# Unread matmuls in TensorE's waits through the whole head, held weight stores, GpSimd casts and a last store on ScalarE's queue

## The chip, the cores and the metric

The kernel runs on one core of a Trainium2 chip. The metric is device time in microseconds of one execution. The time before is the median of three runs, 546.33 us (545.79 to 549.88).

## What is computed

Three blocks follow each other on a tensor of 2 batches, 768 positions and 512 channels (8 heads of 64):

```python
# windowed attention with a linear distance bias
keep = (pos_k < n_global) | ((rel >= 0) & (rel < n_local))     # n_global 8, n_local 96
a = softmax(where(keep, q @ k.T / 8 - slope[h] * dist, -1e9))
x = (a @ v) in the layout batch, position, channel
# layer norm and a channel MLP of 2048
x = x + relu(norm(x) * g_ln @ w_ch1) @ w_ch2
# token MLP of 256, then a channel MLP of 1536
u = x + (relu(x.T @ w_tok1) @ w_tok2).T
out = u + relu(u @ w_ch1) @ w_ch2
```

## The kernel before, in words

The 12 tiles of 128 positions (x0 to x11, `NTT` = 12) stay in SBUF as f32. `window_tile` (line 400) makes one attention tile: scores of two heads at a time (line 452, f32 matmuls), a biased minimum on VectorE (line 467), the exponential on ScalarE (line 472), a transposition on TensorE (line 477), a copy of the transposed probabilities out of PSUM (line 525, on ScalarE or VectorE as `EVX` says) and the product with V (line 482, f32, for tiles below `SPLIT` = 6; later tiles split the operands into f16 pairs). `norm_ops` does the layer norm and `turn_ops` turns a normed tile by a transposing DMA (line 591). `mlp_ops` is the channel MLP: every product is three f16 matmuls (`mm3`, lines 372 to 374: high by high, high by low, low by high). Groups are of three tiles; the first product with weights (buffers `L` from `xa`, `wa`) needs all three turned tiles of group 0.

The weights arrive as 64-bit words. `Weights.split` loads them (line 166, staging `stg`), casts the top half on ScalarE (line 755, into `fw`), joins it with the shifted lower words on VectorE (line 761, into `wf`), and makes a high half (line 777, ScalarE) and a low half (line 780 on GpSimd or line 783 on VectorE). `Weights.get` stores each finished pair of the channel MLPs to a scratch in DRAM (line 736, 256 KB) and reads it back for later passes (line 726). Nearly all DMAs are issued in order by SyncE (SP), so one whose semaphore hasn't come holds all those behind it.

The order of the instructions is not written by hand. `Plan` simulates the engines with a cost for every operation, a priority, and a latency per engine (`LAT`), and emits the operations in that order. The priorities come from constants (`AHEAD`, `SLOT`, `HEAD`, `DUE`, `EARLY`, `LEAD`, `STORE`, `RELOAD`), and strings such as `LOA1`, `EVX` and `MK1` say which engine takes which operation. In the simulation TensorE runs at half rate when too little was done in the window before, apart from the windows in `WARM`, which are taken as done. In `emit`, until the end of the `WARM` windows, unread matmuls of a zero tile (`keep_busy`, line 106, 256 columns, 0.11 us each in the plan) fill a gap that the simulation shows ahead of a TensorE operation. `WARM` is (1, 8), which ends 22.4 us after the plan's zero; the last such matmuls stand at 26.0 us of the trace. An operation of no cost in `rest` ends the filling; it waits for the second turned tile of group 0. The setup ahead of the plan issues 10 and 3 of them (`BUSY`).

In tiles below `SPLIT`, the first 32 rows of the V and K slots are refilled with the global positions after a tile's last product (lines 546 and 548), since the next tile reads that slot again: from that product to the data's arrival the plan takes 1.2 us (`ISSUE`), 0.3 us for the DMA and 1.8 us (`LAT["S"]`).

`distances` (line 110) and `masks` build the bias tables at the start. `Guard.__init__` writes limits and ones by small GpSimd memsets. At the end the addition of the last tile (a "tail" operation) and the stores of tiles 10 and 11 (`BEHIND`) are issued in a last block on SP, ahead of a branch that repeats all in another precision if the guard's sums say so.

Of the kernel before, what the change touches and what calls it, by code (L numbers as in the profile page):

```python
# [182 lines left out]
class Plan:  # L183
# [3 lines left out]
    LAT = {"T": 0.2, "V": 0.13, "A": 0.15, "G": 0.1, "S": 1.8, "N": 0.0}  # L187
# [212 lines left out]
def window_tile(o, plan, prio, T, slot):  # L400
# [40 lines left out]
    for p in range(4):  # L441
# [88 lines left out]
        if T < SPLIT:  # L530
            op("T", 2 * PVC * n, prio(k + slot["PV"]), pv, r=[(pt, 0), *vkeys], w=[(bvs[p // 2], p % 2)], get=bvs if p == 0 else [])
# [20 lines left out]

    if T >= SPLIT:
# [90 lines left out]
class Guard:  # L644
# [7 lines left out]
    def __init__(self, o, plan):  # L652
        self.o, self.plan = o, plan
        self.n = {k: v[0] for k, v in self.AT.items()}
        nc = o.nc
        c = o.check = o.gp.tile([P, 3, self.N], F32, name="check")
        o.ones = o.gp.tile([P, 2], F32, name="ones2")
        o.half1 = o.gp.tile([P, 3], F16, name="half1")
        o.cnt = o.gp.tile([P, 6], F32, name="cnt")
        o.junk = o.gp.tile([P, 512], BF16, name="junk")  # L660
        for k, (a, b, lo, hi) in self.AT.items():
            for i, y in ((1, lo), (2, hi)):
                plan.op("G", 0.2, GUARD0, lambda i=i, a=a, b=b, y=y: nc.gpsimd.memset(c[:, i, a:b], y), w=[("lim", k, i)])
        for i, y in enumerate((1.0, TINY)):
            plan.op("G", 0.2, GUARD0, lambda i=i, y=y: nc.gpsimd.memset(o.ones[:, i:i + 1], y), w=[("one", i)])
        plan.op("A", 0.3, GUARD0, lambda: nc.scalar.activation(out=o.half1[:, 0:2], in_=o.ones[:], func=AF.Copy), r=[("one", 0), ("one", 1)], w=[("half", 0)])
        plan.op("V", 0.1, GUARD0, lambda: nc.vector.tensor_copy(o.half1[:, 2:3], o.ones[:, 1:2]), r=[("one", 1)], w=[("half", 1)])
# [46 lines left out]
class Weights:  # L714


    def __init__(self, o, plan, keep):
        self.o, self.plan, self.kept, self.keep, self.seen = o, plan, set(), keep, set()

    def get(self, src, prio):  # L720
# [12 lines left out]
        if src[0] in self.keep:  # L733
# [3 lines left out]
            op("S", 1.46, prio + STORE, store, r=[(b, "h"), (b, "l")], w=[("kept", src)])  # L737
# [3 lines left out]
    def split(self, src, prio, dst, key, get=(), r=(), after=()):  # L741
# [342 lines left out]
LOA1 = 'VGGGGGVVVVVVGGGV'
LOB1 = 'GVGVVVVGVGVVVVGV'
LOA2 = 'GGVGGGVVGVGV'
LOB2 = 'VGGGVGGGGVGV'
LOT = 'VVG'
NLO, ULO = 'GGGVVVGGVVVV', 'GGVVVVGVVVGG'
# [53 lines left out]
def rest(o, ctx, attn, fast):  # L1143
# [36 lines left out]
    if fast:  # L1180
        plan.WARM = (1, 8)
# [98 lines left out]
LEADS, FLEAD = -94.61, 405.4  # L1280
F2LEAD = [-24.45, -24.48]
FE, SE = 'VGGVVGVVGGVG', 'GVGVGVVG'
HEAD = 72.86
DUE = [38.89, 17.63, 79.14, 46.98]
EARLY = [-33.75, -24.73, -1.92, 0.28]
LEAD = -148.51
EVAC = 19.77
TOK1 = 19.62
TOKW, TOK0 = 157.31, 177.61
# [5 lines left out]
class WindowAttention:  # L1295
# [8 lines left out]
    def ops(self, o, plan, prio):  # L1304
# [16 lines left out]
        for T in range(1, NTT):  # L1321
            window_tile(o, plan, lambda k, T=T: prio(T, k), T, SLOT)
# [5 lines left out]
class GeneralAttention:  # L1328

# [81 lines left out]
def mixer_kernel(ctx, tc, q, k, v, n_global, n_local, g_ln, w1, w2, wt1, wt2, w3, w4, out):  # L1411
# [20 lines left out]
    near = nc.values_load(flag[0:1, 0:1], min_val=0, max_val=1)  # L1432
# [5 lines left out]
    again = nc.values_load(o.again[0:1, 0:1], min_val=0, max_val=1)  # L1438
# [50 lines left out]
```

## Time and profile before

| what | us |
| --- | --- |
| median of three runs | 546.33 |
| lowest and highest run | 545.79, 549.88 |
| the profiled execution's own time | 550.31 |
| its span in the trace | 548.5 |
| TensorE busy in the span | 536.9 |

The profile names engines PE (TensorE matmuls), PEld (its weight loads), DVE (VectorE), ACT (ScalarE), POOL (GpSimd) and SP (SyncE). PEclk is the clock that TensorE was granted as a share of 2.4 GHz: 0.50 is 1.2 GHz. Matmuls are pipelined, so the durations of several in a row overlap. The stretches of time named below are from the start of the span.

### The profile page before, as it was taken

What the parts mean: (1) busy time and instruction counts of PE and PEld (TensorE: products, weight loads), DVE (VectorE), ACT (ScalarE), POOL (GpSimd) and SP (SyncE); (2) the same over time, 40 slices, a digit from 0 to 9 for tenths busy, and PEclk for the clock granted to TensorE, in tenths of its full rate; (3) what the DMA queues carried; (4) which work ended last, traced back from release to release, by engine and by line L of the source; (5) the groups of instructions that cost most, each with busy time, mean ns of one, the idle gap of its engine ahead of it and who ended that gap; (6) DMA issues with size and microseconds to landing.
All of it is one profiled execution on the core that took longest, in us unless ns stands there. A gap on an engine that the chain in (4) does not pass through costs nothing.

```text
span 548.5 us, 9023 instructions
## 1 busy us (share of the span) xinstructions
PE 536.9 (98%) x3117; PEld 303.2 (55%) x3117; DVE 399.9 (73%) x856; ACT 343.1 (63%) x765; POOL 189.1 (34%) x203
## 2 busy tenths in 40 slices
PE   8989999999999999999999999999999999999995
PEld 6877755656565555554555454454555545554542
DVE  6875895588599875787878877888797786654431
ACT  6987976678776744659875736566855554624210
POOL 2232320134022212456344348534544763231000
PEclk9986999999999999999999999999999999999999
DMA  8895996688968777943775610134893332202012
GB/s 260 246 241 161 258 258 173 200 260 247 291 148 218 163 211 203 334 156 95 201 234 173 214 61 3 56 134 136 212 257 124 125 129 98 75 0 78 2 39 81
DMA packets 99786, 89.94 MB, mean 164 GB/s; under 512 B 59028, under 2 KB 73364, under 8 KB 99732
## 3 DMA queue, kind: packets, MB, share of 16 engines
q1 hardware_dynamic: 99730, 89.29, 56.4%
q8 instruction: 26, 0.43, 0.3%
q14 instruction: 28, 0.23, 0.1%
q10 hardware_dynamic: 2, 0.00, 0.0%
HBM read 61.87 MB, written 17.83 MB: 145 GB/s over the span
## 4 chain that ended last, share of the span: by engine, by line
PE 91%; ACT 3%; DVE 2%; DMA 2%; issue 0%; POOL 0%; ACTq 0%; POOLq 0%
PE L L372 12%; PE L L374 12%; PE L L373 12%; PE L2S L374 9%; PE L2S L373 9%; PE L2S L372 8%; PE S L452 4%; PE k L372 4%; PE k L374 4%; PE k L373 4%; PE k L482 4%; PE T L477 3%; PE tok L373 2%; PE tok L374 2%; PE tok L372 2%; DMA stg<-in_moe_w_ch_dram 1%
## 5 line engine op out<-in xcount | busy, mean ns | idle before, releaser
L372 PE MATMUL L2S<-wb,h 128*128 128x512 f16 x228 | 86.4, 379 | 0.0
L373 PE MATMUL L2S<-wb,h 128*128 128x512 f16 x228 | 86.4, 379 | 0.0
L374 PE MATMUL L2S<-wb,h 128*128 128x512 f16 x228 | 86.4, 379 | 0.0
L900 DVE SCALAR_TENSOR_TENSOR x<-L2S,x 128x512 f32<-128x512 f32 x57 | 39.2, 688 | 45.0 <-PE L2S L374 44.8
L374 PEld LDWEIGHTS <-h 128*128 128x128 f16 x336 | 32.9, 98 | 39.6
L372 PEld LDWEIGHTS <-h 128*128 128x128 f16 x336 | 32.9, 98 | 36.5 <-issue 1.0
L373 PEld LDWEIGHTS <-h 128*128 128x128 f16 x336 | 32.9, 98 | 35.5
L755 ACT ACTIVATE fw<-stg 128x512 f16<-128x512 bf16 x62 | 47.1, 776 | 8.6 <-DMA stg<-in_moe_w_ch_dram 6.1
L834 POOL TENSOR_TENSOR Q<-Q 128x256 f32<-128x256 f32 x36 | 31.9, 885 | 47.1 <-DVE Q L834 47.1
L761 DVE SCALAR_TENSOR_TENSOR wf<-stg,fw 128x512 uint32<-128x512 uint32 x62 | 45.7, 750 | 2.5 <-ACT fw L755 2.4
L472 ACT ACTIVATE ex<-ex,mn 128x256 f32<-128x256 f32 (+1 forms) x96 | 41.8, 482 | 8.0 <-DVE mn L467 7.9
L467 DVE CUSTOM_DVE_ANT_0 ex<-bmh,S 128x256 f32<-128x256 bf16 x80 | 30.4, 415 | 15.1 <-PE S L452 11.3
L372 PE MATMUL L<-wb,h 128*128 128x512 f16 x108 | 41.0, 379 | 0.0
L373 PE MATMUL L<-wb,h 128*128 128x512 f16 x108 | 40.9, 379 | 0.0
L374 PE MATMUL L<-wb,h 128*128 128x512 f16 x108 | 40.9, 379 | 0.0
L834 POOL TENSOR_TENSOR sz<-Q,sz 128x512 f16<-128x512 f32 x18 | 23.7, 1318 | 44.7 <-ACT sz L926 40.6
L372 PEld LDWEIGHTS <-wa 128*128 128x128 f16 x268 | 26.4, 98 | 19.0 <-issue 1.3
L374 PEld LDWEIGHTS <-wa 128*128 128x128 f16 x268 | 26.2, 98 | 17.5 <-DVE wa L783 0.3
L373 PEld LDWEIGHTS <-wa 128*128 128x128 f16 x268 | 26.2, 98 | 17.2
L372 PE MATMUL L<-xa,wa 128*128 128x384 f16 x104 | 34.0, 327 | 0.0
L374 PE MATMUL L<-xa,wa 128*128 128x384 f16 x104 | 33.9, 326 | 0.0
L373 PE MATMUL L<-xa,wa 128*128 128x384 f16 x104 | 33.9, 326 | 0.0
(237 smaller groups left out, 1359.7 us busy)
## 6 DMA issues: line engine op xcount, KB each, us to landing
stg<-in_moe_w_ch_dram SPq DMA_DIRECT2D x56, 512.0 KB, 5.1
wa<-scr_1a SPq DMA_DIRECT2D x24, 256.0 KB, 4.4
wb<-scr_1b SPq DMA_DIRECT2D x24, 256.0 KB, 4.1
scr_1a<-wa SPq DMA_DIRECT2D x16, 256.0 KB, 4.6
scr_1b<-wb SPq DMA_DIRECT2D x16, 256.0 KB, 5.0
K<-in_k_dram SPq DMA_DIRECT2D x12, 256.0 KB, 3.7
Q<-in_q_dram SPq DMA_DIRECT2D x12, 256.0 KB, 4.0
V<-in_v_dram SPq DMA_DIRECT2D x12, 256.0 KB, 5.2
```

The source lines that it names most:

```text
L372: nc.tensor.matmul(ps, ah, bh, start=first, stop=False, **k)
L373: nc.tensor.matmul(ps, ah, bl, start=False, stop=False, **k)
L374: nc.tensor.matmul(ps, al, bh, start=False, stop=last, **k)
L452: nc.tensor.matmul(bs[j].t[:, i, :w], o.Q[r, qs, p + i, :], o.K[r, slots, p + i, :], start=True, stop=True)
L467: nc.vector.tensor_tensor_reduce(out=ex.t[:, j, :w], in0=o.bm0[:, h] if n == 1 else o.bmh[:, h, ms, :], in1=bs[j].t[:, p % 2, :w], scale=- ...
L472: nc.scalar.activation(out=ex.t[:, j, :w], in_=ex.t[:, j, :w], func=AF.Exp, bias=mn.t[:, h:h + 1], scale=-1.0)
L477: nc.tensor.transpose(bt.t[:, j, i, :], ex.t[:, j, i * P:(i + 1) * P], o.ident[:])
L482: nc.tensor.matmul(bv.t[:, 2 * (p % 2) + j], pt.t[:, j, i, :], o.V[:, z, 2 * p + j], start=(i == 0), stop=(i == n - 1))
L755: op("A", 0.66, prio - 2, lambda: nc.scalar.activation(out=fw.t[:, :, 1], in_=stg.t[:, 4:2049:4].bitcast(BF16), func=AF.Copy, scale=2.0 if ...
L761: op("V", 0.6, prio - 1, lambda: nc.vector.scalar_tensor_tensor(out=raw().bitcast(U32), in0=stg.t.bitcast(U32)[:, 1:1024:2], scalar=13, in ...
L834: op(eng, {"G": 0.1 + n * 0.00227, "V": 0.07 + n * 0.00104}[eng], prio, lambda: e.tensor_tensor(out=out(), in0=a(), in1=b(), op=alu), lock ...
L900: n = op("V", 0.6, prio, lambda: nc.vector.scalar_tensor_tensor(out=x[:], in0=b.t[:], scalar=BACK if o.half else 1.0, in1=x[:], op0=ALU.mu ...
```

## The change

- `WARM` goes from (1, 8) to (1, 16), so that the fillers may stand until 49.7 us after the plan's zero, and the operation that ends them waits for the third turned tile of group 0. `BUSY` goes from 10 and 3 to 8 and 4.
- `LAT["S"]` goes from 1.8 to 2.4 us.
- Stores of weights to the scratch wait for the last product of tile 4 (`W.hold`, `LATE` = 3).
- Eight of the 32 casts of line 755 for the first channel MLP go to GpSimd (`FA1`, `FB1`), three of them among the first 16.
- `distances` clips only the last 128 columns before the branch; the other 384 are clipped later in `distant`. The guard's memsets and those of `vb` come after tile 0's last minimum.
- The store of tile 10 is issued ahead of the last addition, that of tile 11 on ScalarE's queue.
- Two loads of a register from a tile come without a check of their range at run time.
- All constants of the plan are new, so the order of the whole program is another one. `EVX` gives the copies of tile 3 to VectorE.

```diff
-    t = tp.tile([P, 4 * P], F32, name="mt")
+    t = o.x[NTT - 4]
...
-    nc.vector.tensor_tensor(out=rel[:], in0=rel[:], in1=t[:], op=ALU.max)
+    nc.vector.tensor_tensor(out=rel[:, 3 * P:], in0=rel[:, 3 * P:], in1=t[:, 3 * P:], op=ALU.max)
...
-    LAT = {"T": 0.2, "V": 0.13, "A": 0.15, "G": 0.1, "S": 1.8, "N": 0.0}
+    LAT = {"T": 0.2, "V": 0.13, "A": 0.15, "G": 0.1, "S": 2.4, "N": 0.0}
...
-                plan.op("G", 0.2, GUARD0, lambda i=i, a=a, b=b, y=y: nc.gpsimd.memset(c[:, i, a:b], y), w=[("lim", k, i)])
+                plan.op("G", 0.05, GUARD0, lambda i=i, a=a, b=b, y=y: nc.gpsimd.memset(c[:, i, a:b], y), r=[("first", 3, 1)], w=[("lim", k, i)])
...
-            op("S", 1.46, prio + STORE, store, r=[(b, "h"), (b, "l")], w=[("kept", src)])
+            op("S", 1.46, prio + STORE, store, r=[(b, "h"), (b, "l")], w=[("kept", src)], after=self.hold)
...
+            top = lambda: stg.t[:, 4:2049:4].bitcast(BF16)
+            if o.half and src[0] == 1 and (FA1 if src[1] == "a" else FB1)[src[2]] == "G":
+                op("G", 1.65, prio - 2, lambda: nc.gpsimd.tensor_scalar(
+                    out=fw.t[:, :, 1], in0=top(), scalar1=2.0 if wide else 1.0, scalar2=None, op0=ALU.mult),
+                   r=[(stg, 0), ("zeros",)], w=[(fw, 0)], get=[fw])
...
-STORE, RELOAD = 44.56, -3.32
+STORE, RELOAD = 41.58, 14.54
...
+FA1 = 'AGGAAAAGAAGAAAGA'
+FB1 = 'AAAAAAAAGGAAAAGA'
...
-BUSY = 10, 3
+BUSY = 8, 4
...
-EVX = 'AAAAAAAAAAAV'
+EVX = 'AAAVAAAAAVAA'
...
-        plan.WARM = (1, 8)
+        plan.WARM = (1, 16)
...
     attn.ops(o, plan, prio)
+    W.hold = attn.done[LATE:LATE + 1]
...
-        plan.op("T", 0.0, 0.0, lambda: setattr(plan, "busy", lambda n: None), r=[(g[0], 1, "h")], w=[(idle, 0)])
+        plan.op("T", 0.0, 0.0, lambda: setattr(plan, "busy", lambda n: None), r=[(g[0], 2, "h")], w=[(idle, 0)])
...
+        store(o, BEHIND[0])
         for x in rest:
             x.fn()
-        for T in BEHIND:
-            store(o, T)
+        store(o, BEHIND[1], "scalar")
...
+        def distant():
+            sl = slice(0, 3 * P)
+            nc.vector.tensor_tensor(out=o.bmt[:, sl], in0=o.bmt[:, sl], in1=o.x[NTT - 4][:, sl], op=ALU.max)
+            may(o, o.bmt, o.col, o.x[NTT - 1][:, sl], 0, 3, False)
+        plan.op("V", 1.7, HEAD0 + 8.0, distant, r=[("first", 1, 1)], w=[("rel",)], lock=True)
...
-    near = nc.values_load(flag[0:1, 0:1], min_val=0, max_val=1)
+    near = nc.values_load(flag[0:1, 0:1], min_val=0, max_val=1, skip_runtime_bounds_check_because="a product of comparisons, 0 or 1")
```

## Rows read from the trace of the kernel before

**Rows 1.** The page: span, and busy time of the engines

```profile
span 548.5 us, 9023 instructions
PE 536.9 (98%) x3117; PEld 303.2 (55%) x3117; DVE 399.9 (73%) x856; ACT 343.1 (63%) x765; POOL 189.1 (34%) x203
```

**Rows 2.** Windows: busy per engine (instructions), PEclk, share of DMA engines, GB/s

```profile
5.00:27.00 22.00, 21.88 (x166) 17.70 (x166) 16.68 (x75) 19.83 (x54) 4.06 (x22) 1.00 0.93 273
27.00:53.50 26.50, 24.88 (x145) 20.34 (x144) 18.60 (x62) 20.90 (x43) 9.48 (x14) 0.74 0.77 196
38.00:51.50 13.50, 13.33 (x57) 10.69 (x56) 7.45 (x23) 8.40 (x17) 4.44 (x6) 0.50 0.64 166
53.50:80.00 26.50, 26.50 (x181) 18.27 (x181) 22.25 (x54) 22.24 (x44) 7.46 (x7) 1.00 1.01 281
80.00:543.00 463.00, 460.04 (x2619) 244.82 (x2616) 338.91 (x655) 277.64 (x623) 165.97 (x148) 1.00 0.52 152
```

**Rows 3.** Timeline of TensorE: start, us, instruction, what ended its wait

```profile
19.82 1.04 PE L477 MATMUL T<-ident,ex 128*128 128x128 f32 x8
...
26.00 1.04 PE L106 MATMUL L<-x 128*128 128x256 f16 x8
...
37.26 2.64 PE L482 MATMUL k<-V,pt 128*128 128x65 f32 x14 [1.17 <-DMA V<-in_v_dram]
39.69 1.91 PE L477 MATMUL T<-ident,ex 128*128 128x128 f32 x8
```

**Rows 4.** Timeline of SyncE's DMA issues

```profile
29.67 0.42 SPq L736 DMA_DIRECT2D scr_1a<-wa  x1
32.68 0.64 SPq L548 DMA_DIRECT2D V<-in_v_dram  x1
...
46.98 0.61 SPq L548 DMA_DIRECT2D V<-in_v_dram  x1
47.69 1.28 SPq L591 DMA_TRANSPOSE xa<-xh  x1
...
54.98 2.30 SPq L736 DMA_DIRECT2D scr_1a<-wa  x1
```

**Rows 5.** Groups of ScalarE, 0 to 80 us: busy, mean ns of one

```profile
L525 ACT ACTIVATE pt<-T 128x512 f32<-128x512 f32 (+1 forms) x24 | 12.6, 552 | 4.4 <-PE T L477 4.2
L755 ACT ACTIVATE fw<-stg 128x512 f16<-128x512 bf16 x16 | 12.3, 777 | 1.0 <-DMA stg<-in_moe_w_ch_dram 0.9
```

**Rows 6.** Timeline of VectorE and GpSimd at the start

```profile
2.69 0.69 DVE L125 TENSOR_TENSOR rel<-rel,mt 128x512 f32<-128x512 f32 x1
...
4.82 0.29 DVE L147 TENSOR_TENSOR rel<-rel,mu 128x128 f32<-128x128 f32 x1
...
4.97 0.65 POOL L663 MEMSET check<- 128x31 f32 x12
...
5.03 0.70 DVE L149 TENSOR_SCALAR x<-x,both 128x32 f32<-128x32 f32 x1
```

**Rows 7.** Timeline of GpSimd and VectorE: one input, and side by side

```profile
1.90 0.35 POOL masks.py:199 TENSOR_SCALAR_AFFINE_SELECT ident<-ident 128x128 f32<-128x128 f32 x1
...
28.51 0.69 DVE L761 SCALAR_TENSOR_TENSOR wf<-stg,fw 128x512 uint32<-128x512 uint32 x1
...
37.52 1.33 POOL L631 TENSOR_TENSOR xn<-xn,gB 128x512 f32<-128x512 f32 x1 [0.93 <-ACT xn L624]
37.64 2.36 DVE L761 SCALAR_TENSOR_TENSOR wf<-stg,fw 128x512 uint32<-128x512 uint32 x2
```

**Rows 8.** Waits of SyncE's queue: us in total, times, longest

```profile
SPq L736 <- ACT wb L777: 12.5, 1, 12.5
```

**Rows 9.** Timeline: first issues on two queues, and the last store

```profile
0.74 0.51 ACTq L50 DMA_DIRECT2D nwords<-in_n_local_dram  x1
0.74 0.37 SPq L50 DMA_DIRECT2D nwords<-in_n_global_dram  x1
...
543.17 0.33 SPq L1119 DMA_DIRECT2D out_dram<-x  x1
```

More of the change, by code (lines that the diff above doesn't have):

```diff
@@ L530, in window_tile @@
         if T < SPLIT:
-            op("T", 2 * PVC * n, prio(k + slot["PV"]), pv, r=[(pt, 0), *vkeys], w=[(bvs[p // 2], p % 2)], get=bvs if p == 0 else [])
+            last = op("T", 2 * PVC * n, prio(k + slot["PV"]), pv, r=[(pt, 0), *vkeys], w=[(bvs[p // 2], p % 2)], get=bvs if p == 0 else [])
         if T < SPLIT and p == 3:
@@ L551, in window_tile @@
                    r=[("vb", prev, i) for i in range(2)], w=[("vb", c, i) for i in range(2)])
+    if T < SPLIT:
+        return last
     if T >= SPLIT:
@@ L660, in __init__, with begin @@
         o.junk = o.gp.tile([P, 512], BF16, name="junk")
+    def begin(self):
+        o, plan, nc, c = self.o, self.plan, self.o.nc, self.o.check
         for k, (a, b, lo, hi) in self.AT.items():
             for i, y in ((1, lo), (2, hi)):
-                plan.op("G", 0.2, GUARD0, lambda i=i, a=a, b=b, y=y: nc.gpsimd.memset(c[:, i, a:b], y), w=[("lim", k, i)])
+                plan.op("G", 0.05, GUARD0, lambda i=i, a=a, b=b, y=y: nc.gpsimd.memset(c[:, i, a:b], y), r=[("first", 3, 1)], w=[("lim", k, i)])
         for i, y in enumerate((1.0, TINY)):
-            plan.op("G", 0.2, GUARD0, lambda i=i, y=y: nc.gpsimd.memset(o.ones[:, i:i + 1], y), w=[("one", i)])
+            plan.op("G", 0.05, GUARD0, lambda i=i, y=y: nc.gpsimd.memset(o.ones[:, i:i + 1], y), r=[("first", 3, 1)], w=[("one", i)])
         plan.op("A", 0.3, GUARD0, lambda: nc.scalar.activation(out=o.half1[:, 0:2], in_=o.ones[:], func=AF.Copy), r=[("one", 0), ("one", 1)], w=[("half", 0)])
@@ L717, in __init__ @@
     def __init__(self, o, plan, keep):
-        self.o, self.plan, self.kept, self.keep, self.seen = o, plan, set(), keep, set()
+        self.o, self.plan, self.kept, self.keep, self.seen, self.hold = o, plan, set(), keep, set(), ()
     def get(self, src, prio):
@@ L1076, in token_ops @@
         transpose_ops(o, plan, prio(14 + 2 * i), "uT", lambda T=T: o.x[T][:], [*xk(T), ("tk",), *r], dst, key, get)
-AHEAD = {'s': 16.13, 'k': 39.52, 'q': -12.72, 'v': -109.16}
-STORE, RELOAD = 44.56, -3.32
[L1084 to L1089, printed above, removed]
+AHEAD = {'s': 15.16, 'k': 38.58, 'q': -0.97, 'v': -111.99}
+STORE, RELOAD = 41.58, 14.54
+LOA1 = 'VVVGVGGVVGGVGGVG'
+LOB1 = 'GVGGGGVGVGGVGVGV'
+LOA2 = 'GGGGVVVVVVGG'
+LOB2 = 'GVVVVGVGVVVV'
+FA1 = 'AGGAAAAGAAGAAAGA'
+FB1 = 'AAAAAAAAGGAAAAGA'
+LOT = 'GGV'
+NLO, ULO = 'GVVGVGVVGGVG', 'GGGVVVVVVVGV'
 TURN = 2.2
-PT = 'PDDDPPPPDPPPDDPDDPPDDDDD'
-UP = 66.96
-MK0, MK1, MK2 = 'VVVVAAAA', 'AAAVAAVA', 'AAVVVAAA'
+PT = 'DPDDPDPPPPDDDDPPDDPDDDPD'
+UP = 65.11
+MK0, MK1, MK2 = 'VVVVAAAA', 'AVAVAAAA', 'AVAVAVVV'
 HEAD0 = -200.0
-MASK2 = -178.16
-BUSY = 10, 3
-HOLD = [-139.09, 4.69, -86.88]
+LATE = 3
+MASK2 = -221.83
+BUSY = 8, 4
+HOLD = [-117.53, 7.79, -25.44]
 FIRST = [("k", 0), ("q", 0), ("k", 1), ("q", 1), ("v", 0), (1, "a", 0), ("v", 1), (1, "a", 1), ("k", 2), ("q", 2), (1, "a", 2), ("v", 2)]
@@ L1101 @@
 SPLIT = 6
-PVE = 'AAAVVV'
-EVX = 'AAAAAAAAAAAV'
+PVE = 'VAVAAA'
+EVX = 'AAAVAAAAAVAA'
 QKC, PVC = 0.266, 0.224
-SLOT = {'gk': -97.05, 'exp': 14.41, 'T': -45.19, 'PV': -13.24, 'inv': 3.62, 'st': 37.34, 'xn': 28.12, 'tr': 49.06}
+SLOT = {'gk': -66.36, 'exp': 3.44, 'T': -4.11, 'PV': -45.54, 'inv': -31.26, 'st': 36.85, 'xn': 39.98, 'tr': 37.73}
 NACT = range(0, 4)
-START = {"V": 1.1, "A": 1.5, "G": 3.5, "S": 9.0}
+START = {"V": 1.1, "A": 1.1, "G": 3.5, "S": 9.0}
 BEHIND = (10, 11)
@@ L1114, with store @@
 SIZES = {**WIDE, 'hid': 12, 'wa': 8, 'wb': 8, 'wf': 4, 'fw': 3, 'stg': 4, 'xn': 2, 'ph': 3, 'pq': 2, 'xh': 2, 'uh': 2, 'xz': 3, 'sz': 4}
-def store(o, T):
+def store(o, T, queue="sync"):
     b, t = divmod(T, NT)
-    o.nc.sync.dma_start(o.out[b, t * P:(t + 1) * P, :], o.x[T][:])
+    getattr(o.nc, queue).dma_start(o.out[b, t * P:(t + 1) * P, :], o.x[T][:])
 def rest_pools(o, ctx):
@@ L1279 @@
 BLOCKS2 = [[(c, (0, 1)) for c in range(3)]] * 2
[L1280 to L1289, printed above, removed]
+LEADS, FLEAD = -140.38, 294.54
+F2LEAD = [-56.26, -52.39]
+FE, SE = 'VVGGVVVGGGVG', 'VVGVGVVV'
+HEAD = 65.69
+DUE = [41.01, 16.73, 79.92, 50.05]
+EARLY = [-46.62, -32.02, -2.65, -6.01]
+LEAD = -138.41
+EVAC = 35.88
+TOK1 = -56.64
+TOKW, TOK0 = 165.07, 207.32
 SLOW = dict(SLOT={'gk': -30.97, 'exp': 16.12, 'T': -15.37, 'PV': -13.48, 'inv': 9.01, 'st': 17.62, 'xn': 12.62, 'tr': 1.7}, HEAD=107.54, DUE=[32.9, 21.07, 45.09, 4.38], EARLY=[-15.89, -16.66, 3.92, -16.37], LEAD=21.63, EVAC=3.31,
@@ L1307, in ops @@
         window_tile(o, plan, lambda k: HEAD0 + k, 0, dict.fromkeys(SLOT, 0.0))
-        plan.op("G", 0.3, 20.0, lambda: nc.gpsimd.memset(o.vb[:, :, :, 0, D:], VSC), w=[("vb", z, 0) for z in range(3)])
-        plan.op("G", 0.5, 20.0, lambda: nc.gpsimd.memset(o.vb[:, :, :, 1, D:], 0.0), w=[("vb", z, 1) for z in range(3)])
-        plan.op("V", 1.25, HEAD0 + 8.0, lambda: may(o, o.bmt, o.col, o.x[NTT - 1][:, :3 * P], 0, 3, False), r=[("first", 1, 1)], w=[("rel",)], lock=True)
+        o.guard.begin()
+        plan.op("G", 0.1, 20.0, lambda: nc.gpsimd.memset(o.vb[:, :, :, 0, D:], VSC), r=[("first", 3, 1)], w=[("vb", z, 0) for z in range(3)])
+        plan.op("G", 0.1, 20.0, lambda: nc.gpsimd.memset(o.vb[:, :, :, 1, D:], 0.0), r=[("first", 3, 1)], w=[("vb", z, 1) for z in range(3)])
+        def distant():
[3 more added lines that the diff above has]
+        plan.op("V", 1.7, HEAD0 + 8.0, distant, r=[("first", 1, 1)], w=[("rel",)], lock=True)
         for (d, e, at), engs in zip(((0, 2, HEAD0 + 8.1), (2, 3, MASK2)), (MK1, MK2)):
@@ L1320, in ops @@
                 plan.op(engs[h], cost, at + 0.5 * h, fn, r=[("rel",)], w=[("bm", h, z) for z in range(d, e)], lock=engs[h] != "A")
-        for T in range(1, NTT):
-            window_tile(o, plan, lambda k, T=T: prio(T, k), T, SLOT)
+        self.done = [window_tile(o, plan, lambda k, T=T: prio(T, k), T, SLOT) for T in range(1, NTT)]
     def close(self):
@@ L1328 @@
 class GeneralAttention:
+    done = ()
     def __init__(self, o):
```

8 lines of the change are left out of this document (4 added, 4 removed).

## Prediction

> **What bounds the kernel now.** I read the page's first part, then busy time by windows, then the timeline where a window stands out, then each engine's groups. The page says that TensorE is busy for 536.9 of 548.5 us [rows 1]: only 11.6 us are idle, so what can be won is either that or matmuls that run slowly. The windows show both at one place. From 80 to 543 us TensorE waits for 2.96 us in all (463.00 less 460.04) and has its full clock; from 53.5 to 80 us it never waits. But from 27 to 53.5 us its mean clock is 0.74, and between 38 and 51.5 us it is 0.50, which is 1.2 GHz, with TensorE busy for 13.33 of 13.5 us [rows 2]. The timeline shows what came before: TensorE stood for 1.17 us until 37.26 us for the global rows of V, and soon after it eight transpositions take 1.91 us instead of the 1.04 us that the same eight took at 19.82 us [rows 3]. The last fillers stand at 26.00 us [rows 3]; there is none in the slow stretch. So the stage from 27 to 53.5 us is where the change aims. The work done there at half clock would take 6.67 us less at full clock, and TensorE's work of the stage is then 24.88 less 6.67, some 18.2 us in 26.5.
>
> In that stage SyncE's queue also stands behind TensorE: its copy of V is issued at 46.98 us, when tile 3's product is done, and the last turn of group 0 (`xa`), which is next in the queue, only at 47.69 us [rows 4]. The first weight matmul needs that turn. Faster products let both go earlier.
>
> **The change part by part.**
>
> *Fillers through the head.* If the clock stays up, TensorE needs 18.2 us and is no longer what ends last; ScalarE is busy for 20.90 us of the stage and VectorE for 18.60 us [rows 2]. The change itself moves some of that. Three of the first 16 casts (0.777 us each [rows 5]) leave ScalarE, of which about one by proportion falls into this stage, and tile 3's four copies at 0.55 us [rows 5] go to VectorE, where I take 0.65 us each (the nearest VectorE pass over 512 columns took 0.69 us [rows 7]). ScalarE: 20.90 - 0.78 - 2.2 = 17.9. VectorE: 18.60 + 2.6 = 21.2. So the stage can't go below 21.2 us by this count, a gain of 5.3 us; and engines are not busy all the time. In the stage ahead ScalarE reached 19.83 of 22 us, 90% [rows 2]; 21.2 at 90% is 23.5 us, a gain of 3.0 us. I take 4.0 us, between the two. Ends: nothing if the clock falls all the same, 6.7 us if the plan moves VectorE's work out of the stage as well.
>
> *Price of the fillers.* Eight took 1.04 us, some 0.11 us each behind the first [rows 3]. With 18.2 us of work in about 22.5 us there is room for up to 4.3 us of them, about 39. Each stands in a wait of the plan, and costs only where the real wait is shorter. The nearest measure of that error is the V copy: issue at 32.68 us, data at 37.26 us [rows 3, 4], 4.6 us where the plan before counts 3.3 us and the new one 3.9 us. The plan errs to the short side there, so fillers end too early rather than too late. I take a loss of 0.3 us, ends 0 and 1.5.
>
> *Start.* The maximum over 512 columns took 0.69 us; over 128 columns such a pass took 0.29 us; so 0.40 us leave the path to the branch [rows 6]. A VectorE pass over 32 columns took 0.70 us beside GpSimd's memsets, though one over 128 took 0.29 us; with the memsets gone 0.4 us more goes [rows 6]. The other 384 columns (0.4 to 0.6 us) come back after tile 0's minima, where VectorE is busy for 16.68 of 22 us [rows 2]: hidden; without that cover the start gains only 0.2 us. The two range checks are a few register instructions, which the profile does not count as busy: 0 to 0.4 us. Sum: a gain of 0.7 us, ends 0.1 and 1.2.
>
> *ScalarE before 27 us.* It is 90% busy there [rows 2]. Some two of the moved casts fall here, 1.55 us; I take half as gain, 0.8 us, ends 0 and 1.6.
>
> *Casts on GpSimd.* The trace has no one-input pass over 512 columns there. From below, a one-input pass over 128 columns took 0.35 us; from above, a two-input pass over 512 columns took 1.33 us [rows 7]; four times the first, 1.4 us, is near that, and I take 1.3 us. GpSimd has 9.48 us of work in 26.5 [rows 2], so its own time is covered. But VectorE pays: two passes that take 0.69 us each alone took 2.36 us beside a GpSimd multiplication, 0.98 us more [rows 7]. The GPSIMD Engine Reference of the Trainium skill (section 8, Key points) says the same of two-input VectorE instructions, as a shared interface to SBUF. By that rule each of the casts can stretch VectorE's work, which decides the head in my count; the plan keeps the two apart by a lock, and so I set nothing here and keep it as a rival.
>
> *Stores held back.* Three stores of 256 KB fall before tile 4's end (the first at 29.67 us, the third at 54.98 us) [rows 4]. DMA engines are 0.77 busy in the slow stage, so little is freed; from 53.5 to 80 us they are at 1.01 and move 281 GB/s [rows 2], where three more need 2.8 us. Most loads there are ahead of their use, so I take a loss of 0.4 us, ends 0 and 2.8.
>
> *Tail.* The last store's issue takes 0.33 us on SyncE; at the start ScalarE's queue took 0.51 us where SyncE's took 0.37 us [rows 9]. ScalarE has nothing left then. Zero, with 0.3 us either way. The other store is issued no earlier, since its data come when they came.
>
> *The new order after the head.* TensorE's work is the same, and waits are 2.96 us from 80 us on [rows 2]. They can go or double: zero, ends -1.5 and +3.
>
> Sum: -4.0 + 0.3 - 0.7 - 0.8 + 0.4 = -4.8 us, counted in the profiled execution: 550.31 - 4.8 = 545.5 us by its own clock. That execution is 3.98 us above the median of 546.33 us. I see no row that says where the runs differ; I carry the difference over whole: 546.33 - 4.8 = 541.5 us. If faster runs have a shorter slow stretch, part of the 4.0 us is already theirs.
>
> **The rivals.**
>
> A is the forecast: clock kept, 541.5 us (538 to 544.5).
>
> B, the clock falls all the same. For it: the plan places fillers by its own waits, and the wait ahead of the fall was 1.3 us longer than planned (4.6 against 3.3 us), still 0.7 us longer than in the new plan. Against it: with fillers up to 26 us the clock held through waits of the same kind. Start and ScalarE remain: 546.33 - 1.5 + 0.7 = 545.5 us.
>
> C, GpSimd's casts hold VectorE up. Three casts in the head at 0.98 us raise its floor from 21.2 to 24.1 us; the stage then gains 2.4 us at most, less some waits 1.5: 546.33 - 1.5 - 1.5 + 0.7 = 544.0 us. For it the pair of 2.36 us, against it the lock.
>
> D, everything goes right: the stage gains 6.5 us, start and ScalarE 2.4 us, later waits 0.5 us, and fillers and stores cost 0.4 us: 546.33 - 9.0 = 537.3 us.
>
> E, slower: a held store blocks SyncE's queue. Its wait stands in the same order as the loads of the next tiles; once already a store waited for 12.5 us [rows 8], and everything behind it with it. The stores now wait for a product of tile 4, so one that the plan puts too early stops loads in the stretch where TensorE has no wait at all [rows 2] and DMAs are full. Loads are some 4.6 us ahead by the landing of V; a wait of 12.5 us then costs 7.9 us of TensorE, and the stage's gain is lost with it: 546.33 + 7.9 - 1.5 = 552.7 us. It decides from a new wait of 4.8 us on (no gain) and from 10.3 us on all told is slower by 1%; below that it only eats the gain. Against it: the plan simulates this queue too, and counts 1.46 us for each store.
>
> **How the numbers follow.** A 0.58, B 0.16, C 0.05, D 0.12, E 0.09. A measurement of this kernel tells about 1% from no change: below 540.9 us is faster, above 551.8 us slower. Half of A lies below 540.9 us: 0.29, with D 0.41 faster. The other half with B and C, 0.50, is within 1%; E, 0.09, is slower. The range from 536.5 to 547.5 us takes in D, B and the upper ends of fillers and stores, and leaves out E. A's own range is 538 to 544.5 us.
>
> **What would show it.** Right: zero-tile matmuls between 27 us and the first weight matmul; granted clock 1.00 from 10 us on; eight transpositions at 1.04 us throughout; the first weight matmul some 5 us earlier than 53.5 us, the rest shifted by as much; VectorE, not TensorE, busy longest in that stage. Wrong for B: a clock of 0.50 in some window before 55 us. For C: `wf` passes above 0.8 us beside GpSimd's casts. For E: a store's wait of over 5 us on SyncE's queue ahead of 80 us, and TensorE idle right behind it. The forecast as a whole is wrong if TensorE's waits after 55 us exceed 6 us, since then the new order and not the clock sets the time.

## The result and the profile after

The changed kernel takes 554.12 us (median of six runs, 551.49 to 555.73) against 545.71 us before on the same chip (544.68 to 549.88): a ratio of 1.0135 [1.0093, 1.0177], slower, where 541.5 us was forecast and the range ended at 547.5 us. The medians lie 8.4 us apart; the ratio, with its 95% interval, is estimated from all runs. Two of the six runs had a mean clock of 0.999 and took 551.49 and 551.77 us, the four at 0.996 took 553.80 to 555.73 us. The profiled execution took 554.44 us, its span is 552.6 us. The page of after, busy time of the engines, beside [rows 1]:

```profile
span 552.6 us, 9142 instructions
PE 537.0 (97%) x3162; PEld 302.3 (55%) x3162; DVE 415.1 (75%) x894; ACT 336.6 (61%) x755; POOL 155.2 (28%) x177
```

Windows of after, for the stretches of [rows 2] and the late part (the columns are those of [rows 2]):

```profile
27.00:53.50 26.50, 24.04 (x192) 19.82 (x191) 22.46 (x66) 20.71 (x40) 12.29 (x16) 0.99 1.03 259
53.00:56.50 3.50, 3.50 (x17) 2.44 (x16) 3.02 (x10) 2.76 (x7) 2.47 (x2) 0.51 0.99 321
53.50:80.00 26.50, 26.50 (x177) 18.81 (x177) 17.99 (x51) 18.69 (x39) 7.59 (x8) 0.94 0.84 236
80.00:250.00 170.00, 170.00 (x1089) 95.45 (x1088) 126.85 (x299) 109.89 (x251) 57.70 (x51) 1.00 0.77 209
250.00:500.00 250.00, 244.70 (x1291) 126.15 (x1290) 207.98 (x354) 155.55 (x349) 67.54 (x67) 1.00 0.43 128
```

The half clock is gone from the stretch that the change aimed at (0.99 in place of 0.74); 3.5 us at 0.51 are left, later. TensorE's timeline of after, fillers of line 106 and the first weight matmul:

```profile
34.15 3.23 PE L106 MATMUL L<-x 128*128 128x256 f16 x28
...
38.08 0.44 PE L477 MATMUL T<-ident,ex 128*128 128x128 f32 x2 [0.48 <-ACT ex L472]
...
46.74 0.34 PE L372 MATMUL L<-xa,wa 128*128 128x384 f16 x1
...
52.48 1.49 PE L482 MATMUL k<-V,pt 128*128 128x65 f32 x8 [1.20 <-ACT pt L525]
```

There are 48 fillers between 27 us and 43.7 us. At the pace of the 28 (3.23 us, 0.115 us each) they take 5.5 us. So of the 24.04 us that TensorE is busy in the stage some 18.5 us are the kernel's own work (an estimate by that pace). The first weight matmul stands at 46.74 us, 6.9 us ahead of the profile of before; yet the run is longer.

One filled wait can be followed to its end. The rows below are from the issues of SyncE, then from the chain of waits (start, us), then from ScalarE's timeline, all of after:

```profile
28.94 1.53 SPq L166 DMA_DIRECT2D stg<-in_moe_w_ch_dram  x3
```

```profile
29.58 7.28 DMA stg<-in_moe_w_ch_dram
```

```profile
36.88 0.79 ACT L766 ACTIVATE fw<-stg 128x512 f16<-128x512 bf16 x1 [1.54 <-DMA stg<-in_moe_w_ch_dram]
```

Three loads of weights are issued together at 28.94 us, where the DMA engines are full (1.03 in the window); one lands after 7.28 us. The new order has put a cast of those weights on ScalarE ahead of the exponentials that TensorE's transpositions at 38.08 us need, so ScalarE stands for 1.54 us, and TensorE does 28 unread matmuls and two transpositions and then waits 0.48 us more.

### The profile page after: what moved, and what is told of

The parts are those of the page before. It is cut to its first block, busy times and chain, and to the rows that moved or that the text cites. A ratio compares the mean times of both kernels' runs of the same rounds, so it can differ in the third digit from the quotient of the medians.

```text
span 552.6 us, 9142 instructions
## 1 busy us (share of the span) xinstructions
PE 537.0 (97%) x3162; PEld 302.3 (55%) x3162; DVE 415.1 (75%) x894; ACT 336.6 (61%) x755; POOL 155.2 (28%) x177
## 4 chain that ended last, share of the span: by engine, by line
PE 83%; DVE 8%; DMA 3%; ACT 2%; issue 1%; SPq 1%; POOL 0%; ACTq 0%; DVEq 0%
PE L L372 12%; PE L L373 11%; PE L L374 11%; PE L2S L374 8%; PE L2S L373 8%; PE L2S L372 8%; PE k L372 4%; PE k L374 4%; PE k L373 4%; PE S L452 3%; DMA stg<-in_moe_w_ch_dram 3%; PE k L482 2%; PE T L477 2%; PE tok L372 2%; PE tok L373 2%; PE tok L374 2%
## 5 line engine op out<-in xcount | busy, mean ns | idle before, releaser
L472 ACT ACTIVATE ex<-ex,mn 128x256 f32<-128x256 f32 (+1 forms) x96 | 42.8, 481 | 13.5 <-DVE mn L467 13.0
L766 ACT ACTIVATE fw<-stg 128x512 f16<-128x512 bf16 x54 | 41.0, 776 | 12.2 <-DMA stg<-in_moe_w_ch_dram 6.5
L910 DVE SCALAR_TENSOR_TENSOR x<-L,x 128x512 f32<-128x512 f32 x27 | 18.6, 687 | 20.8 <-PE L L374 20.6
```

The source lines that it names most:

```text
L472: nc.scalar.activation(out=ex.t[:, j, :w], in_=ex.t[:, j, :w], func=AF.Exp, bias=mn.t[:, h:h + 1], scale=-1.0)
L766: op("A", 0.66, prio - 2, lambda: nc.scalar.activation(out=fw.t[:, :, 1], in_=top(), func=AF.Copy, scale=2.0 if wide else 1.0), r=[(stg, 0 ...
L910: n = op("V", 0.6, prio, lambda: nc.vector.scalar_tensor_tensor(out=x[:], in0=b.t[:], scalar=BACK if o.half else 1.0, in1=x[:], op0=ALU.mu ...
```

## The experiments

**The base and the fillers.** Before was run again, unchanged, as a control. Its own text:

> The kernel before, unchanged, with the clock of every run. If the runs of before near 545.5 us have a shorter stretch at half clock than the profiled one (mean clock 0.986 at 550.3 us), they show 0.990 or more here, and most of the clock's gain was there already. If the clock has nothing to do with it, runs at 545 and at 550 us show the same 0.986.

It took 546.08 us (ten runs; 1.0015 [0.9979, 1.0051]). Windows of its profiled run (the fastest of the ten, 545.2 us), its first weight matmul on TensorE's timeline, and a load of weights from the issues of SyncE:

```profile
27.00:53.50 26.50, 24.12 (x181) 19.31 (x180) 20.57 (x67) 25.90 (x53) 12.25 (x16) 1.00 0.93 245
53.50:80.00 26.50, 26.50 (x179) 17.36 (x178) 23.41 (x61) 20.77 (x46) 5.49 (x5) 1.00 0.94 253
80.00:250.00 170.00, 170.00 (x1083) 95.44 (x1080) 129.34 (x298) 116.06 (x258) 49.21 (x43) 1.00 0.78 213
250.00:500.00 250.00, 247.88 (x1315) 128.42 (x1314) 191.40 (x317) 153.28 (x343) 115.59 (x104) 1.00 0.44 128
```

```profile
48.51 0.33 PE L372 MATMUL L<-xa,wa 128*128 128x384 f16 x1
```

```profile
29.19 0.35 SPq L166 DMA_DIRECT2D stg<-in_moe_w_ch_dram  x1
```

This is the row that the prediction lacked. The same program, with no filler after 27 us, has its full clock through the whole head: span 543.4 us, clock 0.998. The profile on which the prediction was built is a rare case: of the 29 runs of before listed with this set of kernels, 24 took 544.2 to 546.8 us and only five more than 547 us, three of them (550.2, 550.75 and 552.12 us) at a mean clock of 0.99 or less, as the execution with 550.31 us at 0.986 had been. In the usual run TensorE does 24.12 us of real work between 27 and 53.5 us, and what is full there is ScalarE, 25.90 of 26.5 us. Against that the changed kernel, with some 18.5 us of real work in the same stretch, loses 5.6 us where 4.0 us were to be won. The load of 29.19 us lands after 6.4 us here, nearly as late as the one of 7.28 us in after; but between 27 and 41 us ScalarE has no wait for a load in the control. The wait in after comes from the place of the cast in ScalarE's order more than from a slower load.

Next, the changed kernel in its own order with its fillers ended where before ends them:

```diff
-        end, until = 0.0, self.TICK * self.WARM[1] - self.ORIGIN
+        end, until = 0.0, self.TICK * min(self.WARM[1], 8) - self.ORIGIN
```

> The kernel after in its own order, but with fillers only up to 22.4 us of the plan, as before. Theory 1 (the new order costs, the fillers only keep the clock): 553 to 560 us, with 0.50 in more windows ahead of 60 us. Theory 2 (the fillers themselves delay TensorE by about 0.11 us each): 547 to 549 us.

It took 555.0 us (1.016 [1.0121, 1.0199]). Its windows:

```profile
27.00:53.50 26.50, 22.27 (x125) 18.46 (x125) 19.61 (x54) 16.95 (x33) 8.94 (x11) 0.71 0.86 204
38.30:55.30 17.00, 16.80 (x70) 13.07 (x71) 10.86 (x31) 8.68 (x17) 5.90 (x6) 0.50 0.72 181
```

On TensorE's timeline the waits that the 28 fillers had covered are now open:

```profile
35.91 0.44 PE L477 MATMUL T<-ident,ex 128*128 128x128 f32 x2 [1.19 <-ACT ex L472]
38.49 0.69 PE L477 MATMUL T<-ident,ex 128*128 128x128 f32 x2 [2.15 <-ACT ex L472]
```

Without these fillers TensorE stands for 4.23 us of the stage (26.5 less 22.27; 2.46 us in after), and the clock falls for 17 us in this profile, which took 558.28 us; the runs at a mean clock of 0.996 took 553.1 and 553.7 us. In the new order the fillers do what they are for and are not what costs the time; the waits that they fill, 3.34 us at this one place, are there without them.

The reverse, before's own order with the fillers carried on to 45 us:

```diff
-        end, until = 0.0, self.TICK * self.WARM[1] - self.ORIGIN
+        end, until = 0.0, self.TICK * 2 * self.WARM[1] - self.ORIGIN
...
-                    r=[(g[0], 1, "h")], w=[(idle, 0)])
+                    r=[(g[0], 2, "h")], w=[(idle, 0)])
```

> The kernel before in its own order, with fillers up to 49.7 us of the plan (some 31 more). Theory 1: 542 to 546 us, no run near 550 us, clock 0.997 or more. Theory 2: 31 times 0.11 us longer, 548 to 549 us. Also possible: the clock falls all the same, 545 to 550 us.

It took 546.71 us (ten runs; 1.002 [0.9995, 1.0046]), above the 546 us that the first theory allowed, and with one run at 551.31 us still among them. In the median there was nothing to gain: the usual run keeps its clock anyway. Whether the fillers help the few runs at a lower clock, ten runs don't tell.

**Single parts of the change in the changed kernel.** First the eight GpSimd casts, issued on ScalarE with everything else in place:

```diff
-                lambda: nc.gpsimd.tensor_scalar(
-                    out=fw.t[:, :, 1], in0=top(), scalar1=2.0 if wide else 1.0, scalar2=None, op0=ALU.mult),
+                lambda: nc.scalar.activation(
+                    out=fw.t[:, :, 1], in_=top(), func=AF.Copy, scale=2.0 if wide else 1.0),
```

> The kernel after in its own order, but the eight casts that went to GpSimd are issued on ScalarE at the same place of the order. If GpSimd's casts (1.67 to 2.00 us each) and their contention with VectorE delay the head: 550 to 553 us. If they cost nothing, or ScalarE's 6.2 us more cost as much: 553 to 556 us.

It took 554.06 us (1.0151 [1.0116, 1.0185]), as after. The profiled run had a mean clock of 1.000 and still a span of 551.4 us, 8.0 us more than the control's, so the loss doesn't need the half clock. Nor do the casts make it by being on GpSimd: at a mean clock of 0.999 or more three runs took 553.17 to 554.37 us, where after took 551.49 and 551.77 us. That casts on GpSimd cost something that ScalarE's longer work here makes up for, as the text allows, is not excluded.

Then the changed kernel with the engine strings of before for the late phases (`LOA2`, `LOB2`, `LOT`, `FE`, `SE`, `NLO`, `ULO`), planned anew, since TensorE's waits from 250 to 500 us had grown from 2.12 us in the control (250 less 247.88) to 5.30 us:

```diff
-LOT = 'VVG'
+LOT = 'GGV'
...
-FE, SE = 'VGGVVGVVGGVG', 'GVGVGVVG'
+FE, SE = 'VVGGVVGGGVVG', 'VVGVGVVV'
```

> The kernel after with the strings of before that share out the second half's work between VectorE and GpSimd (LOA2, LOB2, LOT, FE, SE, NLO, ULO); the planner orders anew. Theory 1 with VectorE as the cause of the late waits: TensorE's waits from 250 to 500 us fall from 5.3 to 2 to 3 us and the time to 550 to 552 us. If the constants' order causes them: 553 to 556 us and waits as they were.

It took 552.76 us (1.0126 [1.0094, 1.0157]). The late waits went (2.10 us from 250 to 500 us), and others came between 80 and 250 us (2.24 us, and 3.4 us at half clock), where the changed kernel has none. VectorE's share could still be the cause of the late waits. Two kernels parted share and order: the changed kernel's order with before's engines for the late differences and halves, and before's order with the changed kernel's engines. The order was simulated with the first letter of each pair and issued on the second:

```diff
-        e = {"G": nc.gpsimd, "V": nc.vector}[eng]
+        e = {"G": nc.gpsimd, "V": nc.vector}[eng[-1]]
...
-    op(lo_eng, {"V": 0.6, "G": 1.26}[lo_eng],
+    op(lo_eng[0], {"V": 0.6, "G": 1.26}[lo_eng[0]],
```

> The kernel after in its own order on all engines, but the second half's sums and differences run on the engine (VectorE or GpSimd) that the strings LOB2, LOT, FE, SE, NLO and ULO of before name. If VectorE's larger share is what makes the late waits: TensorE's idle time from 250 to 500 us falls from 5.3 to 2 to 3.5 us and the time to 551 to 552.5 us. If the order makes them: 5 us stay, 553.5 to 556 us.

> The reverse: the kernel before in its own order, with these operations on the engines that the strings of after name. If VectorE's share makes the late waits: TensorE's idle time from 250 to 500 us rises from 2.1 to 4 to 5.5 us, 547.5 to 549.5 us. If the order makes them: 545.5 to 547 us.

They took 554.69 us (1.0139 [1.0085, 1.0192]) and 547.58 us (1.0025 [0.9995, 1.0055]). The late window of the first, and then of the second:

```profile
250.00:500.00 250.00, 243.76 (x1285) 125.42 (x1284) 198.06 (x314) 155.16 (x348) 113.91 (x105) 1.00 0.43 128
```

```profile
250.00:500.00 250.00, 247.27 (x1310) 127.88 (x1309) 207.01 (x355) 152.25 (x342) 64.43 (x65) 1.00 0.43 128
```

VectorE works 198 us in the one with 6.24 us of waits and 207 us in the one with 2.73 us (2.12 us in the control). By the waits the late ones belong to the order, and the theory of VectorE's share falls. Two things keep this from being clean: in the first kernel operations moved to GpSimd take longer there (a two-input pass over 512 columns took 1.33 us beside VectorE's 0.69 [rows 7]), which can make waits of its own, and the time of the second, 547.58 us, lies just inside the range of the theory that falls (547.5 to 549.5 us).

**Code apart from constants.** The change has two halves: code, and a new set of nearly all planning constants. One kernel has all the code with the constants of before, the other the code of before with all the constants of the change:

```diff
-STORE, RELOAD = 41.58, 14.54
+STORE, RELOAD = 44.56, -3.32
...
-HEAD = 65.69
+HEAD = 72.86
...
-LEAD = -138.41
+LEAD = -148.51
```

> All code of the change, with every constant of the planner as before (latency, priorities, engine strings, BUSY). Order theory (the new constants' order and engine shares cost the 8 us): 545 to 549 us. Feature theory (GpSimd casts, held stores or fillers cost them): 551 to 556 us.

> The code of before with every constant of the change (LAT S 2.4 too), without its fillers, GpSimd casts, held stores or tail. Order theory: 551 to 557 us, with TensorE's waits from 250 to 500 us near 5.3 us. Feature theory: 544 to 548 us.

They took 555.69 us (1.0159 [1.0121, 1.0198]) and 568.41 us (1.0396 [1.0361, 1.0431]). The second has no fillers past 22.4 us of the plan, and its clock in the head falls:

```profile
29.30:66.80 37.50, 34.45 (x142) 27.00 (x143) 21.19 (x64) 20.60 (x41) 8.85 (x13) 0.50 0.72 210
```

By the texts above the first time speaks for the features, and the second fits neither theory. The pair can't part them: either half alone is slow, either brings another order, and the waits stand at different places (the first waits 2.6 us between 80 and 250 us and is at half clock in two stretches of 3.4 us).

**Single parts of the change in before.** The held stores, the GpSimd casts and the new start, each put into before with before's constants. The order is planned anew in each:

```diff
-            op("S", 1.46, prio + STORE, store, r=[(b, "h"), (b, "l")], w=[("kept", src)])
+            op("S", 1.46, prio + STORE, store, r=[(b, "h"), (b, "l")], w=[("kept", src)], after=self.hold)
...
+    W.hold = attn.done[3:4]
```

> The kernel before with one part of the change, the weights' stores held back until tile 4's last product; constants as before, so the planner orders anew (its order differs on all engines). If the held stores cost the head by themselves: 549 to 556 us, with TensorE's lag at 80 us up by 3 us or more. If they don't: 545 to 547 us.

> The kernel before with one part of the change, eight casts on GpSimd; constants as before, a new order. If the casts cost: 549 to 556 us. If not: 544 to 547 us.

> The kernel before with one part of the change, the start (clipping of 384 columns and memsets after tile 0's minima, with the planner's costs and dependences of the change); constants as before, a new order. If this part costs: 549 to 556 us. If not: 544 to 547 us.

They took 555.55 us (1.0181 [1.0143, 1.0219]), 555.35 us (1.0166 [1.0129, 1.0203]) and 550.72 us (1.0115 [1.007, 1.016]). Of the first two, the window after the head and the waits of TensorE in it for the held stores, and the slow stretch in the head for the casts:

```profile
80.00:250.00 170.00, 164.06 (x1040) 92.22 (x1039) 124.97 (x286) 108.14 (x245) 43.25 (x39) 0.99 0.74 209
```

```profile
PE L L374 <- DVE wa L785: 2.7, 1, 2.7
PE L L372 <- DMA wa<-scr_1a: 1.5, 1, 1.5
PE PV L497 <- ACT ao L518: 1.3, 1, 1.3
```

```profile
36.60:46.80 10.20, 9.56 (x42) 8.00 (x44) 4.76 (x14) 7.83 (x17) 4.43 (x5) 0.50 1.01 238
```

Each small edit costs 5 to 10 us, which no cost of the edit itself explains: eight casts of 1.7 us on an engine with half its time free don't make 9.7 us. For the held stores the edit may have a part of its own: pieces of its chain are a store of weights and its read-back,

```profile
110.87 5.68 DMA scr_1a<-wa
116.57 2.73 DMA wa<-scr_1a
```

but its head keeps the full clock with 25.58 of 26.5 us busy from 27 to 53.5 us, so the head's loss in after is not what held stores bring by themselves. With the casts the head loses its time as in after. Pieces of the chain, and the rows of ScalarE and TensorE:

```profile
29.17 6.85 DMA stg<-in_moe_w_ch_dram
```

```profile
36.05 0.78 ACT L761 ACTIVATE fw<-stg 128x512 f16<-128x512 bf16 x1 [0.60 <-DMA stg<-in_moe_w_ch_dram]
```

```profile
37.23 0.69 PE L477 MATMUL T<-ident,ex 128*128 128x128 f32 x2 [1.29 <-ACT ex L472]
```

Two loads are issued together from 28.69 us on, where the control issues one, and a cast that stays on ScalarE waits for the second, ahead of exponentials that TensorE needs. So here the eight casts act through the order that the plan makes of them. With the start, 1.8 us of TensorE's waits from 27 to 250 us are for copies of V; their cause was not followed. That pointed to the order, and the next kernel tries it without any part of the change.

**The order alone.** Three kernels are the code of before with one to three constants moved by 0.5 to 2 us:

```diff
-STORE, RELOAD = 44.56, -3.32
+STORE, RELOAD = 46.56, -1.32
...
-LEAD = -148.51
+LEAD = -150.51
```

> The kernel before with no part of the change, but three constants moved by 2 us (STORE 46.56, RELOAD -1.32, LEAD -150.51), so that the order differs on all engines. If the constants of before are fitted so closely that any other order costs several us (fit theory): 548 to 556 us. If orders near by are as good: 545 to 547 us.

It took 553.43 us (1.0124 [1.0083, 1.0165]; four runs, 550.5 to 554.16 us), about as slow as the whole change. Its windows, the waits of TensorE from 80 us on, and pieces of its chain:

```profile
80.00:129.70 49.70, 47.51 (x344) 28.70 (x340) 34.39 (x101) 37.47 (x92) 9.78 (x10) 1.00 0.80 215
129.70:139.90 10.20, 8.51 (x32) 4.30 (x30) 7.76 (x25) 8.01 (x18) 5.47 (x5) 0.50 0.70 211
```

```profile
PE L L372 <- DMA wa<-scr_1a: 1.7, 1, 1.7
PE PV L497 <- ACT ao L518: 1.0, 1, 1.0
```

```profile
117.97 6.30 DMA stg<-in_moe_w_ch_dram
...
131.03 3.36 DMA wa<-scr_1a
```

The control has 49.70 of 49.70 and 10.20 of 10.20 us busy in these two windows, at full clock. Here a load that takes 6.30 us and a read-back of 3.36 us stand on the chain; 3.9 us of waits (2.19 and 1.69) and half of the 8.51 us at half clock make 8.1 us, and the profiled span is 9.0 us longer than the control's. This profile is of the slowest of the four runs; the fastest, at a mean clock of 0.999, took 550.5 us, so some 5 us of the loss stand without the half clock. It is one order, made by three constants (those of the stores and read-backs among them) but different on every engine, and no sample of all orders; none of it is the change. The other two were a constant each, `HEAD` at 73.86 and `EVAC` at 19.27:

> The kernel before with one constant of the planner moved a little (HEAD 72.86 to 73.86), nothing else; the planner orders anew. If the constants are fitted to one order so closely that any new order costs several us (fit theory), 548 to 556 us. If orders near by are as good and a feature of the change makes the difference, 544.5 to 547 us.

> The kernel before with another constant moved a little (EVAC 19.77 to 19.27), nothing else. Fit theory: 548 to 556 us. Feature theory: 544.5 to 547 us.

They took 545.97 us (1.0001 [0.9984, 1.0018]) and 546.46 us (1.0022 [0.9991, 1.0053]). Their order came out as that of before (TensorE's, GpSimd's and SyncE's rows follow each other as in the control), so they are two more repeats and tell nothing of a new order.

The plan's own latency for DMAs had gone from 1.8 to 2.4 us. It was set back in the changed kernel:

```diff
-    LAT = {"T": 0.2, "V": 0.13, "A": 0.15, "G": 0.1, "S": 2.4, "N": 0.0}
+    LAT = {"T": 0.2, "V": 0.13, "A": 0.15, "G": 0.1, "S": 1.8, "N": 0.0}
```

> The kernel after with the planner's DMA latency at 1.8 us as before instead of 2.4 us, all else as after. If the longer latency is what puts tile 3's scores and minima behind weight passes in the head: 549 to 552 us, with TensorE's lag at 80 us some 2 to 4 us less. If any new order is worse (fit theory): 554 to 562 us.

It took 557.0 us (1.0209 [1.0175, 1.0243]). Its windows of the head and after it:

```profile
27.00:53.50 26.50, 25.25 (x207) 21.00 (x205) 23.52 (x73) 22.32 (x44) 10.94 (x16) 1.00 0.95 247
...
80.00:250.00 170.00, 166.53 (x1052) 93.04 (x1050) 124.30 (x292) 107.16 (x242) 58.69 (x50) 0.99 0.76 205
```

The head is fuller than in the changed kernel, as expected (25.25 us less 42 fillers of 0.115 us leave 20.4 us of own work, against 18.5); 3.47 us of new waits between 80 and 250 us and a stretch of 3.4 us at half clock take more than that back.

**What can be kept.** The last two stores alone, in before's order:

```diff
+        store(o, BEHIND[0])
         for x in rest:
             x.fn()
-        for T in BEHIND:
-            store(o, T)
+        store(o, BEHIND[1], "scalar")
```

> The kernel before with only the two last stores changed (tile 10 ahead of the last addition, tile 11 on ScalarE's queue). From the end of the last matmul to the end of the span there were 6.0 us before and 5.3 us after: if the store's queue is the cause, 0.7 to 0.8 us less than before, 544.8 us; by my prediction nothing, 545.6 us.

It took 544.47 us (twelve runs) beside 545.81: 0.9975 [0.9959, 0.9991], 1.3 us faster. The last rows of its timeline, and then those of the control:

```profile
538.97 0.69 DVE L900 SCALAR_TENSOR_TENSOR x<-L2S,x 128x512 f32<-128x512 f32 x1 [1.90 <-PE L2S L374]
539.69 0.39 ACTq L1119 DMA_DIRECT2D out_dram<-x  x1
```

```profile
537.22 0.69 DVE L900 SCALAR_TENSOR_TENSOR x<-L2S,x 128x512 f32<-128x512 f32 x1 [1.90 <-PE L2S L374]
537.94 0.33 SPq L1119 DMA_DIRECT2D out_dram<-x  x1
```

The spans end at 544.3 and 543.4 us: 5.3 us after the last addition's start with ScalarE's queue, 6.2 us with SyncE's. The issue begins as soon after the addition in both; where behind it the 0.9 us are saved isn't shown. With the cheaper start added in the order of before (the clipping of 384 columns made late, the small memsets deferred, no range checks of the two registers):

> The kernel before in its own order with the parts of the change that need no new order: last stores as in the change, clipping of 384 columns after the branch, guard memsets later, no range checks. The tail gave 1.3 us alone. Prediction: the start's 0.7 us add to it, 543.8 us. If the start is hidden behind ScalarE: 544.5 us.

It took 544.62 us (twelve runs, two of them near 549 us at a clock of 0.99; 0.9983 [0.9962, 1.0005]), no better than the tail alone. The version to keep is before with its last two stores changed.

## Why the prediction was wrong

**The step that failed first: "I carry the difference over whole".** The sum was made in an execution with 13.5 us at half clock, and 3.98 us above the median. No row told what the other runs had, and the prediction said so; the other branch, that "part of the 4.0 us is already theirs", was the case, and more than a part: the control has no slow stretch at all, and fillers in before's order gained nothing. The mechanism was right (half clock after a wait, and fillers that prevent it, shown by the kernel with few fillers beside after), but its price in the usual run is zero. That leaves 541.5 + 4.0 = 545.5 us.

**The step that failed second: "The new order after the head ... zero, ends -1.5 and +3".** It was sized by before's waits after 80 us, 2.96 us, as if these were what any order has. Moving three constants without any part of the change costs 7.8 us by the medians, and the seven other kernels that were planned anew (with the held stores, the casts, the start, either half of code and constants, the DMA latency, the late strings) have medians of 550.7 to 568.4 us. Among these orders that of before is the exception, and the new one is like the others. The same holds inside the head, where the order was taken only as a move of work between engines, with the busiest engine at 90% as the limit: in after the busiest, VectorE, has 22.46 of 26.5 us, 85%, and the wait followed above is ScalarE's for a load. Account of after against the control, profile by profile: up to 80 us TensorE waits for as long in both (4.4 us) and has 9.3 us of fillers ahead of 27 us in both, but after has 5.5 us of fillers more and 1.7 us lost to half clock (half of 3.5), 7.2 us by this estimate. The windows from there to the last matmul, of after and then of the control:

```profile
80.00:547.30 467.30, 461.42 (x2618) 244.46 (x2616) 353.07 (x689) 275.33 (x622) 125.24 (x118) 1.00 0.52 150
```

```profile
80.00:537.20 457.20, 455.07 (x2585) 241.91 (x2581) 334.99 (x642) 274.19 (x611) 164.80 (x147) 1.00 0.53 152
```

After has 6.4 us more of work left at 80 us (461.42 less 455.07), near the 7.2 us, and waits 3.8 us more from there on (5.88 against 2.13), 3.2 of them between 250 and 500 us; the tail gives 0.9 us back. That makes 9.3 us, and the spans differ by 9.2.

**The other terms.** The price of fillers was right: they are harmless, and the waits under them are what costs. GpSimd's casts had their size wrong and their cost right: the group of them in after, up to 250 us,

```profile
L762 POOL TENSOR_SCALAR fw<-stg 128x512 f16<-128x512 bf16 x8 | 13.8, 1725 | 15.9 <-DMA stg<-in_moe_w_ch_dram 14.5 <-ACT bmh L1335 1.2
```

took 1.73 us each, over the upper bound of 1.33 us, but setting them back on ScalarE gained nothing, so rival C was rightly held small. Its sign, longer `wf` passes on VectorE, is hardly to be seen. The group up to 80 us, of after and then of the kernel with the casts on ScalarE:

```profile
L771 DVE SCALAR_TENSOR_TENSOR wf<-stg,fw 128x512 uint32<-128x512 uint32 x15 | 10.8, 740 | 3.3 <-issue 2.0 <-ACT fw L766 1.3
```

```profile
L771 DVE SCALAR_TENSOR_TENSOR wf<-stg,fw 128x512 uint32<-128x512 uint32 x15 | 10.2, 705 | 3.7 <-issue 3.7
```

That is 740 against 705 ns, 0.5 us over the 15 passes, with the casts kept apart by the plan's lock. The Trainium skill (GPSIMD Engine Reference, section 8, Key points) names contention of GpSimd with VectorE instructions that have two SBUF inputs, as these have; these 0.5 us are the most that the rows can show of it. The start's 0.7 us is not to be seen (544.62 beside 544.47 us); that ScalarE, which is full behind it in the control (25.90 of 26.5 us), hides it would fit and was not tested. ScalarE's 0.8 us before 27 us was not tried alone. The tail, set at zero with 0.3 us either way, gained 1.3 us. The held stores' 0.4 us can't be told from the new order that they bring.

Two readings of the prediction were off besides. The 4.6 us from the issue of the V copy to its landing is not a lead of loads over their use, since TensorE stood 1.17 us for that very copy [rows 3]; and E's thresholds of 4.8 and 10.3 us count each microsecond of a store's wait as lost, though the same paragraph takes 4.6 us off.

**The rivals and the signs named.** E had the direction and not the mechanism. The longest waits of SyncE's queue at a store of weights, over the whole run of after (us in total, times, longest):

```profile
SPq L741 <- DVE wa L793: 23.7, 8, 11.1
```

In the list of that queue's waits up to 80 us no store of line 741 stands, and TensorE has no idle time from 53.5 to 80 us. B's sign, half clock before 55 us, came, but in 3.5 us alone (53.0 to 56.5 us), behind the wait of 1.20 us. Of the signs given as right, the fillers, the earlier weight matmul and VectorE as the engine with most real work (22.46 us beside TensorE's 18.5) all came, and the time still rose. They were signs of the head, measured against the slow profile: against the control the first weight matmul is 1.8 us earlier, not 6.9. The sign that should have caught it, "TensorE's waits after 55 us exceed 6 us", was set on the right thing, but from 55 to 547.3 us they come to 5.9 us, all from 80 us on, and it was blind to the head's waits, since a filler counts as busy.

**What stays open.** Why a particular wait arises in each of these orders was followed only for the ones in the head of after and of the kernel with the casts and for the one in the kernel with three constants. So that the order makes the loss is shown by an order without the change that loses as much, and not wait by wait for the new order. Why the same program keeps its clock in most runs and not in some was not settled; the control waits up to 1.00 us in the head and keeps it, the first profile waited 1.17 us and lost it. The changed kernel's order with a single operation moved by hand was not tried, and in that order neither the held stores nor the new start was undone.

## What to carry to other kernels

Before a stall is priced, compare the profiled run's time and clock with those of all runs: a stretch that only the profiled run has is worth nothing in the median. Where a planner makes the order, constants that suit one order need not suit another (here a new order without any part of the change cost 7.8 us); change the code with the order kept, measure that, and measure a new plan as a change of its own, with an order without the change as its control. Once waits are filled with unread work, busy time no longer shows them: subtract the fillers.

## What the runs showed of the hardware

The clock of one program differs from run to run: 29 runs of before had mean clocks from 0.982 to 0.999. A GpSimd cast of 128x512 from bf16 to f16 took 1.73 us, where ScalarE's takes 0.777 us. A last store issued on ScalarE's queue ended the span 0.9 us sooner behind the last addition than on SyncE's (5.3 against 6.2 us), though its issue took 0.39 us and not 0.33.
